# Fourteen transposes of the attention result moved from TensorE to DMA, in an attention and token-mixing kernel on one core

## The chip, the cores and the metric

The kernel runs on one core of a Trainium2 chip. The metric is the time of one execution on the device in microseconds (us), lower is better. Time before: a median of 142.5 us over three runs (142.19 to 142.66).

The engines are TensorE (PE in the profile; its weight loads are shown apart as PEld), VectorE (DVE), ScalarE (ACT), GpSimd (POOL) and SyncE (SP). In this kernel PE does all matrix work, ACT and DVE share what reads PE's results out of PSUM, POOL only issues loads once its constants are built, and SP only issues transfers: a few loads at the start, and all stores. A transfer is issued by an engine's queue in the order of the program and lands some microseconds later.

## The reference

Eight batches, eight heads, 576 tokens, 64 numbers per head. First an attention over a window of 128 tokens, with a bias that falls with the distance; then, on its result `x` of 576 x 512 per batch, a token-mixing layer:

```python
scores = scale * np.matmul(q, k.transpose(0, 1, 3, 2))
mask = (rel >= 0) & (rel < window)                 # rel = query position - key position
scores = np.where(mask, scores + bias[None], -1000000000.0)
attn = np.exp(scores - np.max(scores, axis=-1, keepdims=True))
attn = attn / (np.sum(attn, axis=-1, keepdims=True) + 1e-09)
x = np.matmul(attn, v)                             # heads side by side: batch x 576 x 512
...
wq = x @ w_q                                       # 512 -> 64
wk = x @ w_k                                       # 512 -> 64
W_tok = scale * np.einsum('bsd,btd->bst', wq, wk)
mixed = np.einsum('bst,btd->bsd', W_tok, x)
out = np.maximum(mixed, 0.0) @ w_out               # 512 -> 512
```

Inputs and output are in float32. The kernel works in float16 between PSUM sums.

## The kernel before

**The stages.** Every piece of work is an operation with a short name, a batch and a part. "Part" is a block of 128 tokens (0 to 3; 4 is the tail of 64 tokens) or a group of keys.

For each batch:
- Lq, Lk, Lv load a block of 128 tokens of q, k or v, all heads, from POOL (lines 378 and 391), changing float32 to float16 on the way. Lt loads the 64-row tails of q and k of two batches at once, into the tile natt (line 385).
- TQ transposes a block of q and of k on PE (eight transposes into one PSUM bank); ETQ copies the result to SBUF, on ACT or DVE. TT and ETT do the same with the tails. For batch 0, TF, TJ, EF and EJ stand for them.
- QK multiplies q and k for one group of keys and half of the heads; EXP takes the exponential (ACT, line 591); MUL multiplies by the bias and mask (DVE, line 598). There are 64 of each.
- PV multiplies by v, with a column of ones that gives the sum of each row; RC takes the reciprocal of the sums and X scales by it, which writes the tile x (DVE, lines 652 and 638). Part 4 of two batches shares one tile.

For each group of two batches (0 and 1, 2 and 3, 4 and 5, 6 and 7; operations are named by the first batch):
- XT transposes two x tiles, 128 tokens by 512 each, on PE: eight transposes of 128 x 128 (line 669). EXT copies them into the tile xT (line 675), on ACT or DVE. There are two XT and two EXT for each batch, sixteen in all. XTT and EXTT do the tail.
- WQ, WK and WT multiply xT by the weights; EWQ, EWK and EWT copy the results. WQ and WK of a group need all xT tiles of both batches.
- G forms the 64 x 512 product of wk and x, which replaces the token by token matrix; EG copies it. MX multiplies by wq, RM applies the relu (RMT for the tail), OUT multiplies by w_out, EO copies to an output buffer (tile osb, 15 buffers in rotation), and DO stores it from SP (lines 875 and 878).

CW and CWQ change weights to float16. WM are matmuls on zeros at the start, for the clock.

**The order.** Nothing is left to a scheduler. The string ORDER (lines 48 to 129) lists every operation with the engine that does it and its PSUM bank; each engine executes its own operations in that order, and waits for what an operation depends on. GT entries mark a place after which SP holds the next store back until a given QK is done. The numbers given to `add` (`want` and the engine costs) describe an operation for whoever makes the order; they are not read when the kernel is built.

**What surrounds XT.** X of an even and an odd block come first, then XT, EXT, and WK and WQ behind. An x tile has four buffers by batch (`NX`), so batch 4 overwrites the buffers of batch 0; `add_pv` therefore makes X wait for the XT of four batches before, and `add_xt` makes EXT wait for the WQ and WK of the batch whose xT buffer it overwrites. PE is in order, so an XT that waits for its X holds up whatever follows it on PE.

**Queues.** Both DMA queues use eight semaphores in rotation: each load of POOL, and each transfer of SP, waits for the landing of the one eight before it in the same queue.

Of the kernel before, what the change touches and what calls it, by code (L numbers as in the profile page):

```python
# [45 lines left out]
WARM = (13, 2, 5, 7, 5, 10, 2, 4, 4, 2, 1, 1, 2, 3, 4, 5, 1, 1, 2, 10, 1, 2, 2)  # L46

ORDER = """
warm:D LF0.0.1.1:A LF0.1.0.0:S iota:G WM.0:P01 ident:G wmc:D LF0.0.0.1:S LF0.0.1.0:A ones:D
mask:G LF0.0.0.0:S LF0.1.0.1:S Lq0.2:G bias:A Lk0.1:G zeros:D TF0.1.0:P00 Lt0:G WM.1:P10  # L50
TF0.0.1:P01 EF0.1.0:A biasl:D TF0.0.0:P10 TF0.1.1:P00 WM.2:P20 Lk0.3:G EF0.0.0:A QK0.0.0:P1
EF0.1.1:D Lq0.3:G WM.3:P20 EF0.0.1:D EXP0.0.0:A idh:D Lk0.2:G QK0.0.1:P0 TJ0.2.0:P20 EXP0.0.1:A
TJ0.1.1:P21 EJ0.2.0:D Lk1.3:G WM.4:P30 EJ0.1.1:D MUL0.0.0:D QK0.1.1:P0 Lq1.3:G QK0.1.0:P1
EXP0.1.1:A WM.5:P30 Lq1.2:G EXP0.1.0:A MUL0.1.1:D TT0:P00 Lk1.2:G WM.6:P30 ETT0:D ETT1:A
TJ0.3.1:P01 Lk1.1:G MUL0.1.0:D WM.7:P30 EJ0.3.1:A MUL0.0.1:D TJ0.3.0:P00 Lq1.1:G WM.8:P30
EJ0.3.0:A TJ0.2.1:P01 Lk1.0:G QK0.3.0:P1 EJ0.2.1:D WM.9:P30 EXP0.3.0:A QK0.2.1:P0 Lq1.0:G
WM.10:P30 QK0.3.1:P2 WM.11:P30 EXP0.2.1:A TQ1.3:P10 Lk2.3:G WM.12:P11 ETQ1.3:D EXP0.3.1:A
QK0.2.0:P3 WM.13:P11 Lv0.0:G MUL0.2.1:D TQ1.2:P00 EXP0.2.0:A Lv0.1:G QK1.3.0:P1 ETQ1.2:D
WM.14:P20 EXP1.3.0:A MUL0.3.1:D Lv0.2:G QK1.2.0:P0 TQ1.1:P30 MUL0.2.0:D EXP1.2.0:A Lk2.2:G
QK1.2.1:P1 ETQ1.1:D WM.15:P20 EXP1.2.1:A Lv0.3:G MUL1.2.0:D QK1.1.1:P0 TQ1.0:P30 MUL1.3.0:D  # L60
EXP1.1.1:A Lq2.2:G QK1.1.0:P1 ETQ1.0:D WM.16:P31 QK1.3.1:P2 EXP1.1.0:A WM.17:P31 Lq2.3:G
MUL0.3.0:D PV0.0:P0 QK1.0.0:P3 MUL1.1.1:D EXP1.3.1:A Lv1.0:G MUL1.2.1:D QK1.0.1:P1 EXP1.0.0:A
Lv1.1:G MUL1.1.0:D PV0.1:P2 RC0.0:D EXP1.0.1:A Lv1.2:G X0.0:D PV0.2:P3 RC0.1:D Lk2.0:G X0.1:D
PV0.3:P0 WM.18:P11 RC0.2:D X0.2:D Lv1.3:G TQ2.2:P10 XT0.0:P11 MUL1.3.1:D ETQ2.2:A Lq2.0:G
TQ2.3:P20 MUL1.0.1:D WM.19:P21 ETQ2.3:A Lq2.1:G MUL1.0.0:D RC0.3:D EXT0.0:A PV1.1:P3 X0.3:D
Lk2.1:G QK2.2.0:P2 pads:D PV1.2:P0 RC1.1:D Lv0.4:G EXP2.2.0:A X1.1:D XT0.1:P10 Lv1.4:G wz:D
RC1.2:D QK2.2.1:P3 Lw:S EXT0.1:A X1.2:D PV1.0:P2 Lk3.1:G WM.20:P11 Lwo.2:S RC1.0:D PV1.3:P0
EXP2.2.1:A X1.0:D Lwo.0:S Lq3.1:G WM.21:P11 Lwo.1:S RC1.3:D XT1.0:P10 Lwo.3:S X1.3:D Lt1:G
TQ2.0:P11 EXT1.0:A XT1.1:P00 ETQ2.0:D WM.22:P20 TQ2.1:P01 EXT1.1:D Lq3.0:G PV0.4:P1 ETQ2.1:D
PV1.4:P2 RC0.4:D Lk3.0:G X0.4:D QK2.1.1:P0 QK2.0.0:P3 EXP2.1.1:A Lk3.2:G RC1.4:D QK2.0.1:P1  # L70
X1.4:D Lq3.2:G CWQ:A MUL2.2.1:D QK2.1.0:P0 EXP2.0.0:A XTT0:P20 WK0:P21 Lq4.1:G EXTT0:D
MUL2.1.1:D EXP2.0.1:A Lk3.3:G WT0:P20 EWK0:D WQ0:P30 EWT0:A MUL2.0.0:D Lv2.1:G EXP2.1.0:A G0:P31
EWQ0:D CW.2:A CW.0:D TQ3.1:P10 EG0:A Lq3.3:G CW.1:A ETQ3.1:D MX0.0:P0 MX0.2:P2 RM1.0:A TT2:P11
RM0.2:D RM0.0:A MX0.3:P3 Lt2:G RM1.2:D RM1.3:A MX0.1:P0 ETT2:D RM0.3:A TQ3.0:P10 CW.3:D RM1.1:A
RM0.1:D QK2.3.1:P2 Lv2.0:G OUT1.1:P30 EXP2.3.1:A ETQ3.0:D Lv3.0:G TQ3.2:P31 EO1.1:A MUL2.3.1:D
QK3.0.1:P0 QK2.3.0:P2 Lv2.2:G ETQ3.2:D DO1.1:S EXP3.0.1:A OUT0.3:P10 ETT3:D Lq4.0:G MUL2.0.1:D
EXP2.3.0:A QK3.0.0:P3 QK3.1.1:P0 MUL2.1.0:D Lk4.0:G GT3.0:S OUT1.3:P11 EO0.3:A MUL2.3.0:D
EXP3.1.1:A Lv2.3:G TQ3.3:P20 MUL2.2.0:D OUT1.0:P21 EXP3.0.0:A ETQ3.3:D Lv3.1:G OUT0.1:P10
MUL3.0.1:D EO1.0:A MUL3.0.0:D EO1.3:A QK3.1.0:P0 QK3.3.0:P3 Lk4.1:G MUL3.1.1:D EXP3.1.0:A
QK3.3.1:P2 GT3.1:S GT3.3:S OUT0.2:P11 EO0.1:D Lv3.4:G EXP3.3.0:A MUL3.1.0:D PV2.1:P0 Lv3.2:G  # L80
OUT1.2:P10 EXP3.3.1:A RC2.1:D MUL3.3.0:D Lv3.3:G PV2.2:P3 X2.1:D EO1.2:A QK3.2.1:P2 EO0.2:A
Lv2.4:G RC2.2:D PV2.0:P0 DO1.2:S X2.2:D EXP3.2.1:A OUT0.0:P10 DO0.3:S Lk4.2:G RC2.0:D X2.0:D
TT4:P11 EO0.0:A Lk4.3:G MUL3.3.1:D MX0.4:P3 QK3.2.0:P2 ETT5:A RMT0:D PV3.1:P0 Lq4.3:G GT3.2:S
EXP3.2.0:A XT2.0:P10 MUL3.2.1:D PV2.3:P3 Lq4.2:G RC3.1:D EXT2.0:A MUL3.2.0:D TQ4.0:P20
OUT1.4:P21 RC2.3:D Lq5.3:G X3.1:D ETT4:A ETQ4.0:A X2.3:D PV3.0:P1 TQ4.1:P00 RC3.0:D PV3.2:P3
EO1.4:A X3.0:D Lq5.1:G ETQ4.1:A XT2.1:P01 RC3.2:D X3.2:D XT3.0:P10 Lq5.2:G PV3.3:P2 EXT2.1:A
EXT3.0:D PV3.4:P3 Lq5.0:G RC3.3:D QK4.0.0:P1 X3.3:D PV2.4:P0 Lk5.1:G EXP4.0.0:A GT4.0:S DO1.0:S
RC3.4:D XT3.1:P20 DO1.3:S RC2.4:D Lk5.2:G X2.4:D TQ4.3:P21 EXT3.1:A QK4.0.1:P1 X3.4:D Lk5.3:G
TQ4.2:P00 EXP4.0.1:A WK2:P01 ETQ4.2:D Lk5.0:G ETQ4.3:A XTT2:P20 QK4.1.1:P1 Lk6.3:G EXTT2:D
WQ2:P30 EXP4.1.1:A EWK2:D Lv4.1:G MUL4.0.0:D WT2:P31 EWQ2:D QK4.2.1:P2 EWT2:A QK4.1.0:P0  # L90
EXP4.2.1:A MUL4.1.1:D G2:P10 Lv4.2:G GT4.1:S MUL4.0.1:D EXP4.1.0:A Lk6.2:G QK4.2.0:P3 EG2:D
TQ5.1:P11 EXP4.2.0:A GT4.2:S DO1.4:S Lv4.0:G MX2.0:P0 ETQ5.1:D MX2.2:P2 DO0.1:S RM2.0:A MX2.1:P3
RM3.2:D Lk6.0:G RM3.0:A TQ5.2:P10 RM2.2:D TQ5.3:P11 RM2.1:A Lv4.3:G MUL4.1.0:D RM3.1:A MX2.3:P0
QK4.3.1:P2 RM3.3:A Lq6.0:G ETQ5.3:D TQ5.0:P30 EXP4.3.1:A OUT3.0:P31 ETQ5.2:D Lv5.2:G MUL4.2.0:D
RM2.3:A QK5.3.0:P1 QK5.2.0:P2 ETQ5.0:D EXP5.3.0:A GT5.3:S OUT2.3:P00 GT5.2:S EO3.0:D Lk6.1:G
EXP5.2.0:A OUT3.1:P01 MUL4.3.1:D DO3.0:S MUL4.2.1:D Lv5.1:G EO2.3:A QK5.0.1:P1 QK4.3.0:P3
MUL5.3.0:D EXP5.0.1:A QK5.0.0:P2 Lv4.4:G GT4.3:S OUT2.0:P00 EO3.1:D GT5.0:S EXP4.3.0:A
MUL5.0.1:D Lq6.2:G PV4.2:P1 OUT3.3:P01 EXP5.0.0:A RC4.2:D Lq6.1:G X4.2:D PV4.0:P3 EO2.0:A
MUL4.3.0:D QK5.1.0:P1 QK5.1.1:P2 EO3.3:A RC4.0:D GT5.1:S OUT2.1:P00 Lv5.0:G X4.0:D EXP5.1.1:A
DO3.3:S MUL5.2.0:D TQ6.0:P01 Lq6.3:G EXP5.1.0:A MUL5.1.1:D PV4.1:P3 OUT2.2:P20 Lv5.3:G RC4.1:D  # L100
ETQ6.0:A X4.1:D PV4.3:P1 Lv5.4:G MUL5.1.0:D EO2.2:A QK5.2.1:P3 RC4.3:D Lq7.1:G QK5.3.1:P2
EXP5.2.1:A X4.3:D OUT3.2:P01 MUL5.0.0:D Lk7.0:G EXP5.3.1:A PV4.4:P1 MUL5.2.1:D TQ6.2:P30 Lk7.1:G
RC4.4:D EO3.2:A MUL5.3.1:D XT4.1:P31 ETQ6.2:A PV5.2:P2 X4.4:D Lq7.0:G TQ6.1:P01 EO2.1:A EXT4.1:D
Lt3:G MX2.4:P1 XT4.0:P30 RMT2:A DO2.1:S RC5.2:D TQ6.3:P00 X5.2:D DO2.2:S ETQ6.1:A PV5.1:P1
DO3.2:S ETQ6.3:D DO2.0:S PV5.0:P2 EXT4.0:A Lv6.1:G OUT3.4:P31 RC5.1:D RC5.0:D X5.1:D Lk7.2:G
X5.0:D QK6.0.1:P0 EO3.4:A PV5.3:P1 EXP6.0.1:A Lq7.2:G XT5.0:P20 RC5.3:D X5.3:D PV5.4:P3 EXT5.0:A
Lv6.0:G QK6.1.1:P0 RC5.4:D QK6.2.0:P1 X5.4:D EXP6.1.1:A XT5.1:P21 Lq7.3:G TQ7.1:P20 EXT5.1:D
EXP6.2.0:A Lk7.3:G QK6.2.1:P3 QK6.0.0:P0 MUL6.0.1:D WK4:P21 GT6.0:S EXP6.0.0:A ETQ7.1:D Lv6.3:G
XTT4:P10 MUL6.2.0:D TQ7.0:P11 EXP6.2.1:A QK6.1.0:P0 ETQ7.0:D WQ4:P20 EWK4:A GT6.1:S EXTT4:D
EXP6.1.0:A MUL6.1.1:D WT4:P21 Lv6.2:G MUL6.2.1:D EWQ4:A QK7.0.1:P3 TT6:P10 MUL6.1.0:D EWT4:A  # L110
Lv7.1:G QK7.0.0:P0 EXP7.0.1:A G4:P11 MUL6.0.0:D GT7.0:S DO3.4:S Lv7.0:G ETT6:D EXP7.0.0:A
DO3.1:S QK6.3.1:P2 DO0.2:S EG4:D Lv7.4:G TQ7.2:P30 GT6.2:S EXP6.3.1:A DO0.0:S ETT7:D Lv7.2:G
MX4.2:P0 ETQ7.2:D MX4.3:P1 RM4.2:A MX4.0:P2 RM4.3:D Lv7.3:G RM5.3:A PV6.1:P3 RM5.0:D RM4.0:A
MX4.1:P1 RM5.2:A MUL7.0.0:D Lv6.4:G TQ7.3:P20 RM4.1:A RC6.1:D QK6.3.0:P0 ETQ7.3:D RM5.1:A
OUT4.1:P21 EXP6.3.0:A X6.1:D QK7.2.1:P1 EO4.1:D QK7.3.1:P3 EXP7.2.1:A QK7.2.0:P0 MUL6.3.1:D
OUT5.0:P20 DO4.1:S GT7.2:S GT6.3:S DO2.3:S MUL6.3.0:D EXP7.2.0:A PV6.2:P1 MUL7.0.1:D OUT4.0:P21
EXP7.3.1:A RC6.2:D X6.2:D QK7.1.1:P0 EO5.0:A QK7.3.0:P3 MUL7.3.1:D QK7.1.0:P1 EXP7.1.1:A
OUT5.1:P20 MUL7.2.0:D EXP7.1.0:A MUL7.2.1:D OUT4.2:P00 MUL7.1.1:D EXP7.3.0:A PV6.3:P1 MUL7.1.0:D
OUT4.3:P01 RC6.3:D EO4.0:A X6.3:D EO5.1:A PV7.1:P3 DO4.0:S MUL7.3.0:D EO4.2:A DO5.0:S PV6.0:P1
PV7.2:P2 GT7.1:S EO4.3:A RC6.0:D DO4.2:S RC7.1:D X6.0:D XT6.1:P00 DO5.1:S OUT5.3:P01 DO4.3:S  # L120
RC7.2:D EXT6.1:A X7.1:D GT7.3:S X7.2:D PV7.0:P1 EO5.3:A PV7.3:P3 RC7.0:D XT6.0:P00 X7.0:D
DO5.3:S PV6.4:P2 EXT6.0:A RC7.3:D X7.3:D XT7.0:P01 PV7.4:P1 RC6.4:D EXT7.0:A X6.4:D XT7.1:P30
# [48 lines left out]
def kernel(  # L171
# [111 lines left out]
    def pe(cols, tail=0.0):  # L283
        return {"PE": (cols, cols + 0.17 + tail)}
# [668 lines left out]
```

## Time and profile before

| | |
|---|---|
| median of the runs | 142.5 us (142.19 to 142.66, three runs) |
| the profiled execution, its own time | 142.51 us |
| its span in the profile | 140.4 us |
| busy: PE, DVE, ACT, POOL | 131.1, 117.0, 117.8, 95.6 us |
| last load issued, last landed | 107.0 us, 116.2 us |
| granted TensorE clock | 0.994 |

The page of the profile cuts the span into 40 slices and gives the busy share of each in tenths:

```profile
PE   6999998999898999999999999999899999999970
...
DVE  5866399998998999998899999989979999759330
ACT  4868899697599999998899999999989997748340
POOL 7999999999939998999969688996297000000000
PEclk9999999999999999999999999999999999999997
DMA  4999999999999999999999999999999979205593
```

The slices are 3.5 us each. POOL's row ends at slice 31, with the last load. DMA's row falls soon after. The four rows of the engines are all high from slice 12 on; the last five slices are the output matmuls of the last group, with little for DVE and ACT.

The profiled execution is 142.51 us by the device, and 140.4 us from its first to its last instruction in the profile; the times of the prediction's steps are on the profile's axis, from the span's start.

### The profile page before, as it was taken

What the parts mean: (1) busy time and instruction counts of PE and PEld (TensorE: products, weight loads), DVE (VectorE), ACT (ScalarE), POOL (GpSimd) and SP (SyncE); (2) the same over time, 40 slices, a digit from 0 to 9 for tenths busy, and PEclk for the clock granted to TensorE, in tenths of its full rate; (3) what the DMA queues carried; (4) which work ended last, traced back from release to release, by engine and by line L of the source; (5) the groups of instructions that cost most, each with busy time, mean ns of one, the idle gap of its engine ahead of it and who ended that gap; (6) DMA issues with size and microseconds to landing.
All of it is one profiled execution on the core that took longest, in us unless ns stands there. A gap on an engine that the chain in (4) does not pass through costs nothing.

```text
span 140.4 us, 4614 instructions
## 1 busy us (share of the span) xinstructions
PE 131.1 (93%) x1909; PEld 87.7 (62%) x1909; DVE 117.0 (83%) x270; ACT 117.8 (84%) x168; POOL 95.6 (68%) x118
## 2 busy tenths in 40 slices
PE   6999998999898999999999999999899999999970
PEld 5867655868664556788646566978446568753430
DVE  5866399998998999998899999989979999759330
ACT  4868899697599999998899999999989997748340
POOL 7999999999939998999969688996297000000000
PEclk9999999999999999999999999999999999999997
DMA  4999999999999999999999999999999979205593
GB/s 101 199 151 155 150 151 155 150 152 165 258 225 158 159 195 155 185 212 157 237 161 183 212 197 191 161 216 259 163 170 247 211 169 374 79 0 149 161 389 130
DMA packets 119477, 25.60 MB, mean 182 GB/s; under 512 B 114208, under 2 KB 114464, under 8 KB 119456
## 3 DMA queue, kind: packets, MB, share of 16 engines
q0 software_dynamic: 109264, 13.77, 154.7%
q1 hardware_dynamic: 9136, 11.28, 24.2%
q10 hardware_dynamic: 1056, 0.26, 0.8%
q8 instruction: 15, 0.25, 0.6%
q14 instruction: 6, 0.05, 0.1%
HBM read 29.62 MB, written 9.44 MB: 278 GB/s over the span
## 4 chain that ended last, share of the span: by engine, by line
PE 60%; ACT 15%; DMA 7%; DVE 6%; issue 5%; POOL 3%; ACTq 0%
PE pair L248 49%; PE pair L251 11%; ACT pt L591 10%; DMA natt<-in_k_dram 7%; POOL nat L378 2%; ACT rm L785 2%; DVE qkT L257 2%; DVE pt L598 1%; DVE x L638 1%; DVE osb L257 1%; ACT wout_sb L255 1%; ACT xT L255 1%; DVE inv L652 1%; POOL natt L385 1%; ACT wkt L255 0%
## 5 line engine op out<-in xcount | busy, mean ns | idle before, releaser
L591 ACT ACTIVATE pt<-pair 128x1024 f16<-128x1024 f32 x64 | 62.4, 1045 | 5.1 <-PE pair L248 5.0
L391 POOL DMA_DIRECT2D vt<-in_v_dram x40 | 34.7, 896 | 7.9 <-DMA natt<-in_q_dram 4.5
L598 DVE TENSOR_TENSOR pt<-pt,bias 128x1024 f16<-128x1024 f16 x48 | 31.6, 685 | 1.1 <-ACT pt L591 0.9
L248 PE MATMUL pair<-wout_sb,rm 128*128 128x512 f16 (+1 forms) x132 | 31.4, 373 | 0.0
L378 POOL DMA_DIRECT2D nat<-in_k_dram x31 | 28.8, 945 | 1.5 <-issue 0.5
L378 POOL DMA_DIRECT2D nat<-in_q_dram x30 | 28.1, 968 | 1.7 <-DMA vt<-in_v_dram 0.9
L248 PEld LDWEIGHTS <-pt 128*128 128x128 f16 x576 | 20.8, 97 | 5.8 <-issue 2.5
L248 PE MATMUL pair<-vt,pt 128*128 128x65 f16 x576 | 23.1, 193 | 0.9 <-ACT pt L591 0.8
L248 PE MATMUL pair<-qkT 64*128 64x256 f16 (+2 forms) x320 | 22.4, 250 | 0.8 <-ACT pt L591 0.3
L638 DVE TENSOR_TENSOR x<-pair,inv 128x512 f16<-128x512 f32 x32 | 21.7, 686 | 0.8
L257 DVE COPY qkT<-pair 128x1024 f16<-128x1024 f16 (+1 forms) x28 | 16.8, 611 | 5.3 <-PE pair L251 3.2
L255 ACT COPY osb<-pair 128x512 f32<-128x512 f32 (+1 forms) x28 | 15.9, 609 | 3.8 <-PE pair L248 3.8
L251 PE MATMUL pair<-identh,nat 128*128 128x128 f16 x244 | 18.8, 219 | 0.2
L248 PEld LDWEIGHTS <-rm 128*128 128x128 f16 x132 | 11.4, 97 | 12.0 <-issue 1.3
L251 PEld LDWEIGHTS <-nat 128*128 128x128 f16 x244 | 14.7, 98 | 3.8 <-issue 2.3
L248 PEld LDWEIGHTS <-qkT 64*128 64x128 f16 x320 | 10.9, 94 | 9.2 <-issue 4.0
L248 PE MATMUL pair<-warm 128*128 128x256 f16 x89 | 15.2, 299 | 1.1 <-DVE warm L298 1.1
L255 ACT COPY xT<-pair 128x1024 f16<-128x1024 f16 x12 | 12.1, 1023 | 1.7 <-PE pair L251 1.7
L255 ACT COPY qkT<-pair 128x1024 f16<-128x1024 f16 (+1 forms) x13 | 10.9, 866 | 1.7 <-PE pair L251 1.2
L785 ACT ACTIVATE rm<-pair 128x512 f16<-128x512 f32 x21 | 10.9, 623 | 0.0
L598 DVE TENSOR_TENSOR pt<-pt,biasl 128x1024 f16<-128x1024 f16 x16 | 10.8, 679 | 0.1
L248 PEld LDWEIGHTS <-warm 128*128 128x128 f16 x89 | 8.4, 106 | 4.0 <-issue 1.3
(69 smaller groups left out, 136.9 us busy)
## 6 DMA issues: line engine op xcount, KB each, us to landing
out_dram<-osb SPq DMA_DIRECT2D x31, 256.0 KB, 5.3
vt<-in_v_dram POOLq DMA_DIRECT2D x32, 128.0 KB, 6.9
nat<-in_k_dram POOLq DMA_DIRECT2D x31, 128.0 KB, 6.9
nat<-in_q_dram POOLq DMA_DIRECT2D x30, 128.0 KB, 6.9
out_dram<-osb SPq DMA_DIRECT2D x10, 128.0 KB, 2.5
osb<-in_moe_w_out_dram SPq DMA_DIRECT2D x4, 256.0 KB, 6.5
osb<-in_q_dram SPq DMA_DIRECT2D x4, 128.0 KB, 3.3
natt<-in_q_dram POOLq DMA_DIRECT2D x4, 128.0 KB, 8.1
```

Source lines behind the costliest of these rows:

```text
L248: hold(nc.tensor.matmul(*a, **k))
L251: hold(nc.tensor.transpose(*a))
L255: hold(nc.scalar.copy(out_ap, in_ap))
L257: hold(nc.vector.tensor_copy(out=out_ap, in_=in_ap))
L378: return lambda: nc.gpsimd.dma_start(out=natv(b, j, n), in_=(q, k)[j][b, :, P * n:P * n + P, :].transpose([1, 0, 2]))
L385: nc.gpsimd.dma_start(out=natt_s[pr % 2][:, j].rearrange("p e h d -> p (e h) d"), in_=(q, k)[j][2 * pr:2 * pr + 2, :, 512:576, :].rearrang ...
L391: return lambda: nc.gpsimd.dma_start(out=vtv(b, t)[:n, :, 0:D], in_=v[b, :, P * t:P * t + n, :].transpose([1, 0, 2]))
L591: nc.scalar.activation(out=pt[:, 0:1024], in_=two(s.bank).rearrange("p e c -> p (e c)"), func=AF.Exp, scale=SCALE)
L598: ENG2[o.eng].tensor_tensor(out=pt[:, 0:1024], in0=pt[:, 0:1024], in1=bt, op=ALU.mult)
L638: nc.vector.tensor_tensor(out=x[r].rearrange("p (g h d) -> p g h d", g=2, h=4), in0=sums(p)[r, :, :, 0:64], in1=box["inv"][r].unsqueeze(3) ...
L652: nc.vector.reciprocal(out=box["inv"][r], in_=sums(p)[r, :, :, 64])
L785: hold(nc.scalar.activation(out=out_ap, in_=in_ap, func=AF.Relu, scale=WSCALE))
```

## The change

For seven pairs of x tiles the XT on PE and the EXT on ACT or DVE are replaced by two DMA transposes each, DX, issued by SP: both pairs of batches 4, 5 and 6, and the first pair of batch 7. A DX reads one x tile (128 tokens by 512, float16, 128 KB) from SBUF and writes its four 128 x 128 blocks, transposed, straight into the xT tile in SBUF, without PSUM. It waits for the X of its tile alone. WQ and WK now wait for both DX of a pair in place of one EXT. Nine of sixteen XT and EXT stay as they were. The diff without most of the order:

```diff
-WARM = (13, 2, 5, 7, 5, 10, 2, 4, 4, 2, 1, 1, 2, 3, 4, 5, 1, 1, 2, 10, 1, 2, 2)
+DT = ((4, 0), (4, 1), (5, 0), (5, 1), (6, 0), (6, 1), (7, 0))
+
+WARM = (15, 8, 5, 8, 5, 2, 15, 1, 10, 7, 1, 3, 4, 4, 1, 1)
...
-        old = [gdn.get(GROUP.get(b - NX)), xtd.get((b - NX, qt // 2))]
+        old = [gdn.get(GROUP.get(b - NX)), xtd.get((b - NX, qt // 2)), xtd.get((b - NX, qt // 2, 0))]
...
     def add_xt(b, i, want):
+        if (b, i) in DT:
+            for n in range(2):
+                t = 2 * i + n
+
+                def dx(o, t=t):
+                    nc.sync.dma_start(out=xT_s[b % NX][:, :, P * t:P * t + P], in_=x_s[b % NX][t],
+                                      transpose=True)
+
+                old = [f(gi) for gi in (GROUP.get(b - NX),)
+                       for f in (lambda z: wqd.get((z, 0)), wkd.get)]
+                d = add("DX", b, t, want, {"SP": (0.6, 2.5)}, [xop[b, t], *old], dx)
+                xtd[b, i, n] = d
+            xtd[b, i] = d
+            ext[b, i] = [xtd[b, i, 0], d]
+            return
+
...
-        ext[b, i] = add("EXT", b, i, want + 0.6, EV(1.02, 0.69), [t, *old], ev, frees=[t])
+        ext[b, i] = [add("EXT", b, i, want + 0.6, EV(1.02, 0.69), [t, *old], ev, frees=[t])]
...
-        t = add("WQ", bs[0], "", want, pe(0.5 * nb), [wts, *(ext[b, i] for b in bs for i in range(2))],
+        t = add("WQ", bs[0], "", want, pe(0.5 * nb), [wts, *(e for b in bs for i in range(2) for e in ext[b, i])],
...
-                [wts, *(ext[b, i] for b in bs for i in range(2))], emk, banks=1)
+                [wts, *(e for b in bs for i in range(2) for e in ext[b, i])], emk, banks=1)
```

The whole of ORDER is new, from the first operation on: which engine does which copy, the sequence on every engine, the loads' sequence on POOL and the stores' place on SP. Its two places around the new transposes, DX4.1 to DX5.3 and DX6.1 to DX7.0, with what stands between the last of them and WK6:

```text
PV4.2:P1 RC4.1:D EO2.2:A X4.1:D QK5.0.1:P0 Lv5.3:G EO3.2:A MUL5.2.0:D QK4.3.0:P3 DX4.1:S
EXP5.0.1:A OUT2.1:P20 RC4.2:D Lq7.1:G X4.2:D EXP4.3.0:A PV4.0:P0 MUL5.0.1:D Lk7.0:G DX4.2:S
...
X5.0:D PV5.3:P0 Lq7.2:G ETQ6.3:A TQ7.1:P30 RC5.3:D DX5.0:S X5.3:D QK6.0.0:P2 QK6.2.0:P1
EXP6.0.0:A ETQ7.1:D TQ7.0:P31 Lq7.3:G GT4.3:S DX5.3:S MX2.4:P0 ETQ7.0:D EXP6.2.0:A QK6.1.0:P2
MUL6.0.0:D QK6.1.1:P3 GT5.3:S DO0.0:S EXP6.1.1:A RMT2:D QK6.2.1:P1 MUL6.2.0:D TT6:P00 EXP6.2.1:A
Lv6.0:G PV5.4:P3 ETT7:D ETT6:D EXP6.1.0:A Lv6.2:G QK7.0.1:P1 RC5.4:D PV4.4:P0 X5.4:D EXP7.0.1:A
Lv7.3:G QK7.0.0:P2 RC4.4:D OUT3.4:P30 X4.4:D EXP7.0.0:A MUL6.1.1:D XTT4:P31 Lv7.1:G QK6.3.1:P1
EXTT4:D QK6.0.1:P0 EXP6.3.1:A QK6.3.0:P2 EO3.4:D Lv7.0:G WT4:P31 MUL7.0.0:D WK4:P30 DO3.4:S
...
DX6.3:S X6.0:D EO4.3:A QK7.3.0:P2 OUT5.1:P11 EXP7.3.0:A RC7.0:D MUL7.3.1:D DX6.0:S X7.0:D
PV7.2:P3 EO5.1:A OUT5.3:P10 MUL7.3.0:D DX7.0:S RC7.2:D PV7.3:P0 X7.2:D EO5.3:A PV7.4:P2 RC7.3:D
DO2.0:S X7.3:D PV6.4:P3 DO4.0:S RC7.4:D MX4.4:P1 DO5.1:S X7.4:D XT7.1:P00 RMT4:A GT6.0:S GT6.3:S
GT6.1:S GT5.1:S GT6.2:S DO4.3:S OUT5.2:P01 EXT7.1:A RC6.4:D X6.4:D OUT5.4:P10 XTT6:P00 EO5.4:D
WK6:P11 EXTT6:A WT6:P00 EWK6:A WQ6:P20 EWT6:D EO5.2:D G6:P21 EWQ6:D DO5.2:S DO5.4:S OUT4.2:P30
```

SP issues its transfers in this order: in front of DX4.1 stand all stores of batch 1 and two of batch 0; behind DX5.3 come the eleven remaining stores of batches 0, 2 and 3, of which DO2.0 is the last and stands behind DX7.0. Before the change, SP issued its stores between 47 and 137 us, and nothing else after 35 us. The tail load of batches 6 and 7, Lt3, is the 92nd and 93rd transfer of POOL (94th and 95th before).

## The prediction

> **What bounds the kernel now.** I read the busy time by stretch first, then the chain of waits, then the load queue, then the groups that the change touches. Busy time of each engine in ten-microsecond stretches (stretch, length, then PE, weight loads, DVE, ACT, POOL, each with its instructions; granted clock, DMA share, GB/s):
>
> ```profile
> 80.00:90.00 10.00, 9.97 (x163) 7.10 (x163) 9.64 (x20) 9.94 (x14) 8.57 (x10) 1.00 2.23 185
> 90.00:100.00 10.00, 10.00 (x193) 7.48 (x194) 9.01 (x19) 9.71 (x13) 7.02 (x9) 1.00 2.03 216
> 100.00:110.00 10.00, 9.22 (x130) 5.46 (x130) 8.97 (x18) 9.47 (x17) 6.52 (x8) 1.00 2.02 202
> 110.00:120.00 10.00, 10.00 (x181) 7.22 (x178) 9.79 (x23) 9.02 (x14) 0.00 (x0) 1.00 1.17 262
> ```
>
> Three engines are full at once, at full clock. From 40 to 120 us PE is busy 78.3 of 80, ACT 77.0, DVE 75.2. Relief of one is worth only what the next allows. The chain of waits (start, length, what):
>
> ```profile
> 90.17 0.81 POOL natt L385
> 90.98 10.46 DMA natt<-in_k_dram
> 101.44 0.05 issue
> 101.48 0.35 PE pair L251 x6
> ...
> 106.83 9.66 PE pair L248 x136
> 116.49 0.45 PE pair L251 x8
> 116.94 1.60 PE pair L248 x28
> 118.53 0.45 PE pair L251 x8
> ```
>
> It passes through a load (the 64-row tails of batches 6 and 7, tile natt, which TT6 transposes) and then runs on PE; "L251 x8" behind 116 us is one XT, 0.45 us. POOL, in order of time, shows why loads matter (start, length, what, idle before and what ended it):
>
> ```profile
> 90.98 0.84 POOL L385 DMA_DIRECT2D natt<-in_k_dram  x1
> ...
> 99.90 0.87 POOL L391 DMA_DIRECT2D vt<-in_v_dram  x1 [2.41 <-DMA natt<-in_q_dram]
> 102.04 5.74 POOL L391 DMA_DIRECT2D vt<-in_v_dram  x7 [1.26 <-DMA natt<-in_k_dram]
> ```
>
> A load is issued every 0.9 us and waits for the load eight before it. Its place in the queue, not the engine work, sets when it lands. The last is issued at 107 us.
>
> **The parts, costed.** The rows of what goes and of what stands near it:
>
> ```profile
> L251 PE MATMUL pair<-identh,x 128*128 128x128 f16 x128 | 9.6, 219 | 0.1
> L255 ACT COPY xT<-pair 128x1024 f16<-128x1024 f16 x12 | 12.1, 1023 | 1.7 <-PE pair L251 1.7
> L257 DVE COPY xT<-pair 128x1024 f16<-128x1024 f16 x4 | 2.7, 684 | 0.1
> L638 DVE TENSOR_TENSOR x<-pair,inv 128x512 f16<-128x512 f32 x32 | 21.7, 686 | 0.8
> ```
>
> Removed: 7 XT, 56 of 128 transposes, 7 x 0.45 = 3.2 us of PE; 7 EXT, five on ACT (5 x 1.02 = 5.1 us) and two on DVE (2 x 0.68 = 1.4 us). Added: 14 DMA transposes of 128 KB in SP's queue. The written order deals other copies anew, and what counts is the work ahead of X7.3, the last full tile, behind which the kernel drains. Counting the two orders up to X7.3:
> - PE: 6 XT fewer (2.7), one OUT fewer (0.86): 3.6 us less.
> - DVE: two EXT, two ETQ and one EG fewer (5 x 0.68), one ETT and one EXTT fewer (2 x 0.42); two RM, one EO (3 x 0.68) and one CW (0.42) more: 1.8 us less.
> - ACT: four EXT fewer (4.1), two EO, two RM and one CW fewer (5 x 0.61); two ETQ more (2.0), an EG, ETT and EXTT more (3 x 0.6): 3.3 us less.
>
> The smallest saving decides where all three are full: DVE's 1.8. The same count can be read on the old time axis: I look up when the old execution had done as much of an engine's work as stands ahead of an operation in the new order, and take the latest engine. X7.3 ended at 119.9; the new order gives PE 116.0, DVE 118.2, ACT 116.2, so 118.2. Then PE does XT7.1 (0.45), OUT5.2, OUT5.4 (0.86 each) and XTT6 (0.22), and WK6 starts at 120.6 instead of 122.2. Behind WK6 both orders leave 13 us of PE (OUT4.2 stands where OUT5.4 filled the wait for EG6). Gain 1.6 us.
>
> The front part is reordered too (batch 1's loads ahead of the last of batch 0, 90 warm-up matmuls for 89). G0 ended at 42.0 and comes out at 42.1, so nothing is taken for it; bounds 1 us either way.
>
> DMA transposes: the old trace has none. Two things are to be bounded, the time to landing and the spacing in which one follows another. Issues and landings, 84 to 104 us, then 112 to 124 us:
>
> ```profile
> out_dram<-osb SPq DMA_DIRECT2D x6, 256.0 KB, 6.6
> ...
> out_dram<-osb SPq DMA_DIRECT2D x2, 128.0 KB, 5.2
> natt<-in_q_dram POOLq DMA_DIRECT2D x1, 128.0 KB, 9.4
> natt<-in_k_dram POOLq DMA_DIRECT2D x1, 128.0 KB, 10.5
> ```
> ```profile
> out_dram<-osb SPq DMA_DIRECT2D x6, 256.0 KB, 2.3
> ```
>
> Landing: 5.2 us beside the loads (equal bytes, same queue), upper end 10.5; 2.3 us after them. The last transpose of batches 4 and 5 follows X5.3 (93.5 by the count), WK4 is due at 99.7: 6.2 us of cover, 1.0 to spare; at 10.5 it is 4.3 late. DX7.0 follows X7.0 (116.2), WK6 is due at 120.6: 4.4 us of cover for 2.3. The cover is PE work: OUT3.4 and eight QK there, PV7.3, PV7.4, PV6.4, XT7.1 and two OUT here. Spacing: SP's stores follow one another in 0.4 us, and landed 0.6 to 0.8 us apart after the loads, 1.1 us apart beside them; a transpose has half their bytes in smaller pieces. I take 1.1 us, nearest by queue and size; lower end 0.4, upper end 2.5 (the page's median landing of a 128 KB store, if none overlaps). At 1.1 us, 14 of them are hidden; SP does nothing else.
>
> The Trainium skill speaks against the change: the page "VectorE: DVE Perf Modes", section "The three transpose paths", gives a 128x128 transpose 390 ns on TensorE and 1309 ns by DMA, and advises TensorE where PSUM will do. The first figure isn't what this chain shows (0.45 us for eight, 56 ns each). By the second, as an estimate, a tile's four blocks in a row are 5.2 us; "Advanced Engine Details and Errata", section "X-Bar Transpose (TRN2)", sets them instead near the speed of plain copies, which would leave the sum as it is.
>
> SP's queue: eight transposes now stand ahead of eleven stores of batches 0, 2 and 3. In the old trace six of these, 256 KB each, left between 77.8 and 91.6 us; now they wait for X5.3, and leave beside the last loads of batch 7. So stores leave the loads alone earlier, eight transposes of 128 KB take their place, and the stores come back behind them: I count that as nothing, bounds 3.5 us either way (8 x 0.43, half the issue time of a load, which moves twice the bytes). There are 15 output buffers; the nearest reuse is EO4.2, which needs DO2.0, queued behind DX7.0: issued at 117, landed at 119.5, wanted near 123. If SP ran 3.5 us late, EO4.2 would wait, behind it on ACT RM6.2, and behind that the nine last OUT.
>
> Loads: the tail load stands two places earlier in POOL's queue, so 1.9 us earlier, but TT6 comes at 95.4 instead of 100.5. At the page's median landing for natt (8.0) it lands at 97.1; EXP6.2.1 and EXP6.1.0 carry ACT to 98.4, and QK7.0.1 is through by 98.3. I charge 0.3 us.
>
> Sum: 142.51 (the profiled execution, span 140.4, in line with the median 142.5) - 1.6 + 0.3 = **141.2 us**.
>
> **The rivals.**
> - Tail loads late (no change). Lt3 took 10.5 us in the old trace. Then it lands at 99.5, QK7.0.1 ends at 100.7, ACT stands 2.3 us from 98.4, less the 0.7 us that PE waited before: 141.2 - 0.3 + 1.6 = 142.5. For it: that very row. Against: four 256 KB stores were issued within a microsecond of it, which now wait.
> - Transposes too close to one another (slower). Eight from X4.1 (84.5) to WK4 (99.7) and six from X6.1 (109.1) to WK6 (120.6) allow 1.9 us each. Above that SP's stream sets the end. At 2.5 us they end at 104.5 and 124.1, 4.8 and 3.5 late: 141.2 + 8.3 = 149.5; at 2.2 us, 145.3. For it: nothing in the trace shows a transpose overlapping another. Against: all other transfers of this queue overlap.
> - Four blocks of 128x128 to a tile, one after another (much slower), each at the spacing of a store: 4 x 1.1 = 4.4 us a tile beside the loads, 4 x 0.7 = 2.8 after. Eight end 35.2 us after 84.5, 20.0 late; six end 16.8 us after 109.1, 5.3 late: 166.5. Against it: each transpose is one instruction with one semaphore. By the skill's 1309 ns ("VectorE: DVE Perf Modes", as above) this rival would give some 187 us.
> - PE alone sets the end: all 3.2 us come, 139.3. Against it DVE's 9.79 of 10 in 110 to 120 us.
> - The change not doing what it says: the new order names 14 transposes on SP and 9 XT on PE; nothing is left to doubt.
>
> **How the numbers follow.** Forecast 0.51, its own range 140.3 to 142.0; tail loads 0.19; spacing 0.19; blocks in series 0.03; PE alone 0.08. A measurement here tells 0.3% (0.43 us) from no change, so faster is under 142.07, slower over 142.93. Faster: 0.48 of the forecast, 0.08, and 0.04 of the tail loads, 0.60. Same: 0.03 and 0.09, 0.12. Slower: 0.06, 0.19 and 0.03, 0.28. The range runs from 139.3 (PE alone) to 146.0 (2.2 us of spacing and some more); left out are about half of the spacing case, the blocks in series, and little below.
>
> **What would show it.** Right: DX landings under 6 us beside the loads and near 2.3 after, X7.3 ended near 118, PE without a gap at WK4 and WK6, DVE fuller than before from 100 to 118 us. Wrong: PE idle at WK4 or WK6, ended by a DMA into xT; DX landings spaced over 1.9 us; PE waiting several us for natt at TT6, or ACT idle behind it; EO4.2 waiting for a store.

## The result, and the profile after

The changed kernel takes 148.13 us (median of four runs, 146.91 to 149.17) against 142.52 us: it is 5.6 us slower. Two executions lasted 147 us at a granted clock of 0.994 to 1.0 and two 149 us at 0.985 to 0.987; the slowest is the profiled one (149.17 us, span 147.4), so a microsecond or two of its trace are not part of the comparison, and the ratio, 1.037 with a 95% interval of 1.027 to 1.047, leaves it out (the median of the other three is 147.23 us).

The 40 slices of the page of the changed kernel, 3.7 us each, in tenths:

```profile
PE   7899999867998999999999999989679989999990
...
PEclk9999999999999999999999999999977999999998
DMA  4999999999999999999999999999999999766994
```

Counted from 0, PE has a hole in two places: early, in slices 8 and 9 (29 to 37 us), and in slices 28 and 29 (103 to 110 us). The granted clock falls to 0.7 in slices 29 and 30. DMA stays full to slice 33, 125 us; before it fell behind 119 us. The stretches of ten microseconds show the second hole in numbers (columns as in the prediction):

```profile
90.00:100.00 10.00, 9.31 (x178) 7.19 (x176) 9.72 (x20) 8.82 (x12) 8.16 (x11) 1.00 2.25 129
100.00:110.00 10.00, 7.57 (x130) 4.91 (x128) 7.36 (x16) 7.65 (x12) 5.01 (x6) 0.94 1.81 158
110.00:120.00 10.00, 9.00 (x106) 4.79 (x104) 7.08 (x14) 6.89 (x11) 0.68 (x1) 0.89 1.80 246
```

From 100 to 110 us all three engines idle for more than two microseconds each, so none of them is the bound there. The chain of waits says what is (start, length, what):

```profile
91.99 0.70 POOL nat L379
92.69 10.59 DMA vt<-in_v_dram
103.56 15.55 DMA vt<-in_v_dram
119.16 8.35 PE pair L249 x156
```

Before, this part of the chain passed through one load and came back to PE at 101 us. Now it stays in two loads, one after another, until 119. A load of v that is issued at 103.56 lands 15.6 us later. The transfers issued from 84 to 112 us (KB each, median time to landing), and the first of these lines in the kernel before:

```profile
vt<-in_v_dram POOLq DMA_DIRECT2D x9, 128.0 KB, 13.4
nat<-in_q_dram POOLq DMA_DIRECT2D x5, 128.0 KB, 5.7
...
xT<-x SPq DMA_TRANSPOSE x8, 8.3
```
```profile
vt<-in_v_dram POOLq DMA_DIRECT2D x9, 128.0 KB, 8.4
```

And the packets that the two queues moved from 90 to 110 us, before the change and after it (q0 carries the loads, q1 SP's transfers; packets, MB, share of the engines):

```profile
q0 software_dynamic: 17267, 2.18, 171.8%
q1 hardware_dynamic: 1087, 1.96, 29.4%
```
```profile
q0 software_dynamic: 12507, 1.58, 147.5%
q1 hardware_dynamic: 4272, 1.26, 54.9%
```

In the same 20 us 4760 fewer load packets went through, 4.6 loads at 1024 packets each, although SP moved fewer bytes than before (1.26 MB for 1.96). It moved them in four times as many packets: a transposed tile counts 512 packets of 256 B and 32 of 4 B. The last load landed at 121.5 us; before it was 116.2.

PE's own longest wait for a transfer is for a transpose, and the load of the chain shows with a shorter one (PE's timeline: start, length, idle before in brackets):

```profile
104.50 1.01 PE L249 MATMUL pair<-wqk_sb,xT 128*128 128x64 f16 x28
107.93 0.29 PE L249 MATMUL pair<-wqk_sb,xT 128*128 128x64 f16 x4 [2.42 <-DMA xT<-x]
...
119.16 0.66 PE L249 MATMUL pair<-vt,pt 128*128 128x65 f16 x16 [0.72 <-DMA vt<-in_v_dram]
```

The 28 matmuls of WK4 run, and the last four wait for DX5.3. X5.3 was done at 96.9, but DX5.0 held SP for 3.1 us; DX5.3 was issued at 99.5 and landed at 107.9. The two waits stand for the same time in part. Where the loads are fewer (below), PE comes to the matmul of the last line at 114.5; here it came at 118.4, because of DX5.3 and the clock behind it, and stood 0.7 us more. The load, issued at 103.56 before either wait, would have held it until 119.2 without them.

Ahead of the transposes the kernel is late too: the matmuls of G0 ended at 44.3 us (41.7 before), X3.3 at 66.8 (64.5). X7.3 ended at 127.3 (119.9 before, 118.2 forecast).

### The profile page after: what moved, and what is told of

The parts are those of the page before. It is cut to its first block, busy times and chain, and to the rows that moved or that the text cites. A ratio compares the mean times of both kernels' runs of the same rounds, so it can differ in the third digit from the quotient of the medians.

```text
span 147.4 us, 4515 instructions
## 1 busy us (share of the span) xinstructions
PE 133.3 (90%) x1854; PEld 86.8 (59%) x1854; DVE 116.6 (79%) x268; ACT 115.4 (78%) x163; POOL 95.6 (65%) x118
## 4 chain that ended last, share of the span: by engine, by line
POOL 29%; PE 25%; DMA 24%; DVE 8%; ACT 8%; issue 4%; POOLq 0%; ACTq 0%; DVEq 0%
PE pair L249 22%; POOL nat L379 18%; DMA vt<-in_v_dram 18%; POOL vt L392 8%; DMA nat<-in_q_dram 6%; ACT pt L592 3%; PE pair L252 3%; POOL natt L386 2%; DVE pt L599 2%; ACT xT L256 2%; DVE x L639 2%; ACT osb L256 1%; DVE rm L804 1%; ACT qkT L256 1%; DVE wout_sb L258 1%
## 5 line engine op out<-in xcount | busy, mean ns | idle before, releaser
L258 DVE COPY qkT<-pair 128x1024 f16<-128x1024 f16 (+1 forms) x25 | 15.0, 612 | 9.2 <-PE pair L252 8.9
L252 PE MATMUL pair<-identh,nat 128*128 128x128 f16 x244 | 19.3, 222 | 0.4 <-DMA nat<-in_q_dram 0.2
L256 ACT COPY osb<-pair 128x512 f32<-128x512 f32 (+1 forms) x26 | 14.5, 593 | 5.6 <-PE pair L249 4.0
L256 ACT COPY qkT<-pair 128x1024 f16<-128x1024 f16 (+1 forms) x16 | 13.6, 863 | 3.0 <-PE pair L252 3.0
L249 PE MATMUL pair<-warm 128*128 128x256 f16 x90 | 14.1, 298 | 1.4 <-DVE warm L299 1.1
L249 PEld LDWEIGHTS <-warm 128*128 128x128 f16 x90 | 8.9, 106 | 3.9 <-issue 1.3
L258 DVE COPY osb<-pair 128x512 f32<-128x512 f32 (+1 forms) x11 | 7.3, 663 | 3.8 <-PE pair L249 3.6
L802 ACT ACTIVATE rm<-pair 128x512 f16<-128x512 f32 x18 | 9.3, 622 | 0.6 <-PE pair L249 0.6
```

The lines of the kernel that those rows point to most:

```text
L249: hold(nc.tensor.matmul(*a, **k))
L252: hold(nc.tensor.transpose(*a))
L256: hold(nc.scalar.copy(out_ap, in_ap))
L258: hold(nc.vector.tensor_copy(out=out_ap, in_=in_ap))
L802: hold(nc.scalar.activation(out=out_ap, in_=in_ap, func=AF.Relu, scale=WSCALE))
```

## The experiments

Theory A: a DMA transpose costs no engine time but takes the place of about one load in flight; the loads of batches 6 and 7 come late, and the engines wait for them. Theory B: the new order, above all its front, costs the time, whatever does the transposes. In the diffs the first file is the kernel before unless another is named.

**The new order without DMA transposes.** All seven pairs go back to XT and EXT, in the changed kernel's order.

```diff
-DT = ((4, 0), (4, 1), (5, 0), (5, 1), (6, 0), (6, 1), (7, 0))
+DT = ()
```

> The new order with all 14 transposes taken back to PE: 7 XT and 7 EXT (five on ACT, two on DVE) stand where the second transpose of each pair stood. Theory A (the DMA transposes delay the loads beside them, whose landings grew from 5 to 16 us): with no transposes in flight the loads land as before, G4 ends near 106 instead of 112.1 us, and the time falls to 142.5 to 143.5. Theory B (the new order itself loses, since G0 ended 2.6 us and G2 4.2 us late before the first transpose was issued at 87.3 us): the time stays at 146 or more, and with the 3.2 us of PE back rather above 147. If both share the loss, 144 to 145.5.

Measured: 154.55 us (152.50 to 156.47). The loads issued from 84 us on landed in 4.5 to 6 us, the last at 108.8, yet PE waited for copies by ACT and DVE, with X5.3 at 100.3. Where the seven XT and EXT were put is my choice, and it broke the fit of the order; nobody's number was met. What follows is only that this order relies on having no XT there.

**The old order with all 14 transposes**, each right behind its X.

```diff
-RC4.1:D ETQ6.0:A X4.1:D PV4.3:P1 Lv5.4:G
+RC4.1:D ETQ6.0:A X4.1:D DX4.1:S PV4.3:P1 Lv5.4:G
```

> The order of before, with the same 14 DMA transposes, each put on SP right behind the X of its tile, and the 7 XT and 7 EXT taken out; nothing else moves. Theory A: the loads issued from 85 us on land late as in the changed kernel, 12 us and more, and the time is 145 to 147. Theory B: the transposes are hidden, PE, ACT and DVE have less to do, and the time is 141 to 142. Theory C (the last transposes come too late for WK4 and WK6, whatever the loads do): PE waits 2 us and more at WK4 or WK6 for xT, loads land in under 10.5 us.

Measured: 156.52 us (155.12 to 158.02), ratio 1.094 (1.086 to 1.103). Loads issued from 85 to 95 us took 11 to 17 us to land. The waits (us in total, times, longest):

```profile
PEld L251 <- DMA nat<-in_k_dram: 5.6, 1, 5.6
PE pair L251 <- DMA nat<-in_k_dram: 5.4, 1, 5.4
...
PEld L248 <- DMA xT<-x: 3.3, 1, 3.3
```

The larger wait is for a load of k, Lk7.1: it landed in time for TQ7.1, which began at 95.6 us before, and at 105.9 us here. The wait for a transpose, at WK6, is the smaller one. That speaks for A, and against B: the order is the old one.

**The two groups apart**, in the old order: the eight transposes of batches 4 and 5, and the six of batch 6 and 7.0.

```diff
+DT = ((4, 0), (4, 1), (5, 0), (5, 1))
```

> The order of before with 8 DMA transposes alone, those of batches 4 and 5, beside the loads of batches 6 and 7. Theory A: all of the loss of the variant with 14 is here, 144.5 to 147, with the loads issued from 85 to 100 us landing after 10 us and more. Theory B: 141 to 142.5. Theory C: PE waits for xT at WK4 while the loads land as before.

```diff
+DT = ((6, 0), (6, 1), (7, 0))
```

> The order of before with 6 DMA transposes alone, those of batch 6 and of the first pair of batch 7 (X6.1 is at 108 us, the last load is issued at 107). Theory A: hardly a load is left to delay, so the saving of 3 XT (1.4 us of PE) and 3 EXT (3.1 us of ACT) shows: 141 to 142. Theory C: WK6 waits for DX7.0, 143 to 144. Theory B says nothing against it: 141 to 142.

Measured: the eight 151.65 us (ratio 1.065, 1.058 to 1.072), the six 148.49 us (1.040, 1.033 to 1.047). The waits of the run with eight, then of that with six:

```profile
PEld L251 <- DMA nat<-in_k_dram: 6.7, 1, 6.7
```
```profile
PEld L248 <- DMA xT<-x: 3.8, 1, 3.8
```

The eight run beside loads, and Lk7.1 takes 16.8 us instead of 6.5. The six hardly touch the loads; there it is SP's queue. X7.0 was done at 120.0 us, but DX7.0 was issued only at 124.8, because DX6.0, two stores and DX7.1 stood ahead of it from 119.5 on, and DX7.1 alone held SP for 2.8 us; WK6, which began at 123, waited. The changed kernel's order avoids that: its WK6 waited for nothing.

All three runs in the old order cost more than Theory A or any other expectation said. One difference of the orders may explain part of it, and no run tests it alone: the changed kernel issues Lk7.1 at 76.7 us, ahead of the transposes, and the old order at 88 to 89 us, among them.

**Four transposes of batch 6 alone, stores behind them**, as a try at a faster version: DO4.0, DO5.0 and DO4.2 are put behind DX6.0.

```diff
+DT = ((6, 0), (6, 1))
...
-PV7.1:P3 DO4.0:S MUL7.3.0:D EO4.2:A DO5.0:S PV6.0:P1
+PV7.1:P3 MUL7.3.0:D EO4.2:A PV6.0:P1
...
+X6.0:D DX6.0:S DO4.0:S DO5.0:S DO4.2:S DO5.1:S
```

> The old order with only the four transposes of batch 6 on SP (X6.1 at 108 us, X6.0 at 117) and the stores DO4.0, DO5.0 and DO4.2 put behind the last of them; 2 XT (0.9 us of PE) and 2 EXT (2.0 us of ACT) are gone. With six transposes WK6 waited 3.7 us for the last, whose landing was held up on SP behind stores and other transposes. Theory A and C: here the last one lands at 120, ahead of WK6 at 122, and the time is 141.5 to 142.5, a chance to beat both kernels. If PE's own pace does not change because DVE sets the end there: 142.3 as before. If transposes lose even here: 144 and more.

Measured: 143.63 us (142.20 to 144.20, ten runs), ratio 1.007 (1.003 to 1.011). No wait was left at WK6, and yet nothing was gained: the two EXT that go were ACT's, and X7.3, a step of DVE, came at 120.5 us where it had come at 119.9. Where the small loss comes from is not shown.

**The old front with the new back**: the old order up to ETQ4.3, the changed kernel's from there.

> The old order up to ETQ4.3 (66 us, between the loads of batch 4 and WK2), the new order with its 14 transposes from there on; only five operations are out of the new order's sequence at the seam. The changed kernel ended G2 at 75.9 us, the one before at 71.7. Theory B (the new front of the order loses 4 us and the transposes then lose little more): about 143, that is 147.2 of the changed kernel's undisturbed runs less 4. Theory A (the transposes beside the loads lose it all, and the front's delay is only slack): 147 as the changed kernel.

Measured: 146.99 us (146.84 to 147.87), ratio 1.030 (1.024 to 1.036). G0 is back at 41.7 us, and little is won. The hole and the fallen clock stay (PE and PEclk in 40 slices of 3.6 us, then two of PE's waits):

```profile
PE   7999997999899999998969999985999979999990
...
PEclk9999999999999999999999999998699999999999
```
```profile
99.37 0.40 PE L251 MATMUL pair<-identh,natt 64*128 64x64 f16 x8 [1.04 <-DMA natt<-in_k_dram]
...
117.02 0.66 PE L248 MATMUL pair<-vt,pt 128*128 128x65 f16 x16 [1.00 <-DMA vt<-in_v_dram]
```

PE waits for no transpose in this run, neither at WK4 nor at WK6; its waits for transfers are all for loads, 2.5 us together from 98 us on (and 1.4 us at 74, ahead of the transposes). So the front is at most a small part of the 5.6 us while the loads are late.

**Eight transposes added that nobody reads**, to the kernel before, issued from 34 us on, and **eight plain copies** in their place, in 512 pieces of 256 B each.

```diff
+    for i in range(8):
+        def dd(o, i=i):
+            nc.sync.dma_start(out=xT_s[2 + i // 4][:, :, P * (i % 4):P * (i % 4) + P], in_=x_s[i // 4][i % 4], transpose=True)
```

> The kernel before, with eight added DMA transposes of 128 KB on SP right behind the weights' loads (issued from 35 us on), from x tiles of batches 0 and 1 into xT tiles of batches 2 and 3 that are written again later; nothing reads them. They only take queue and DMA time. Theory A: each displaces about one load (in the changed kernel 236 packets of transposes a us stood for 499 fewer load packets a us, 1075 load packets for a transpose of 512, a load has 1024): the loads behind them land 7 to 8 us later and the time is 147 to 150. If a transpose costs only its packets in the load's currency (half a load): 3 to 4 us later, 145 to 146.5. Theory B: no change, 142.5.

```diff
+            nc.sync.dma_start(out=xT_s[2 + i // 4][:, :, P * (i % 4):P * (i % 4) + P], in_=x_s[i // 4][i % 4].rearrange("p (c t) -> p c t", c=4))
```

> The same as the variant with eight added transposes, at the same place and with the same sources, bytes and number of 256-byte pieces, but as plain copies within SBUF, without transposing. If it is the number of pieces and bytes that displaces loads, the time and the landings are those of the eight transposes. If it is the transposing, the copies cost 2 us or less: 142.5 to 144.5.

Later the same copies in 128 pieces of 1 KB:

```diff
+            nc.sync.dma_start(out=xT_s[2 + i // 4][:, i % 4, :], in_=x_s[i // 4][i % 4])
```

> The kernel before with eight added copies of 128 KB at the same place as the eight dummy transposes, but in 128 pieces of 1 KB each rather than 512 of 256 B; nothing reads them. If the number of pieces is what displaces the loads (Theory A in its sharper form): a quarter of the pieces, so +1.6 to +2.5 us in place of +6.5 us. If the bytes moved decide: +6.5 us again.

Measured, each with its ratio to the kernel before, and the load Lk3.3, which all eight transfers overtake:

| added | time | more | ratio (interval) | Lk3.3 landed |
|---|---|---|---|---|
| nothing | 142.3 us | | | 47.6 us |
| 8 transposes | 150.65 | 8.3 us, 1.04 each | 1.053 (1.045 to 1.061) | 57.3 |
| 8 copies, 256 B | 148.80 | 6.5 us, 0.81 each | 1.044 (1.037 to 1.051) | 54.5 |
| 8 copies, 1 KB | 146.99 | 4.6 us, 0.57 each | 1.033 (1.026 to 1.040) | 51.4 |

No engine does any more work in these kernels, and nothing waits for the added transfers. The packets from 40 to 48 us, in the kernel before and in those with transposes, with 256 B and with 1 KB copies:

```profile
q0 software_dynamic: 9461, 1.19, 235.1%
q1 hardware_dynamic: 37, 0.06, 2.3%
```
```profile
q0 software_dynamic: 3717, 0.47, 106.5%
q1 hardware_dynamic: 1984, 0.51, 74.8%
```
```profile
q0 software_dynamic: 4162, 0.53, 101.0%
q1 hardware_dynamic: 2624, 0.81, 67.4%
```
```profile
q0 software_dynamic: 4565, 0.58, 112.0%
q1 hardware_dynamic: 1276, 1.26, 57.6%
```

In the first block the loads have the DMA engines to themselves. With transposes in flight 5744 load packets are missing for 1984 packets of SP's: one displaces 2.9. Lk3.3 slips by 9.7 us, and the kernel ends 8.3 us later. Theory A's price of a full load for a transpose is met. (PE waits for the late loads, and from 45 to 55 us its granted clock is 0.5 to 0.63; how much of the 8.3 us that makes is not separated. Lk3.3 was issued at 39.5 us, ahead of it.) The rival that bytes alone count falls, as fewer pieces of the same bytes cost less; but a quarter of the pieces costs 0.57 us and not a quarter, so the piece count is not all of it either, and the 1 KB run came out above the 1.6 to 2.5 us expected of it. The transposing itself is the smallest part, 0.2 us, and no more than a hint: the intervals of transposes and 256 B copies overlap.

**Six transposes that nobody reads, after the last load.**

```diff
-DO5.3:S PV6.4:P2 EXT6.0:A
+DO5.3:S DD.0:S DD.1:S DD.2:S DD.3:S DD.4:S DD.5:S PV6.4:P2 EXT6.0:A
```

> The kernel before with six added transposes of 128 KB behind the store DO5.3 (about 118.8 us), after the last load has landed (116.2 us); nothing reads them. Theory A (a transpose costs what it takes away from the loads in flight): no load is in flight, so no more than 0.5 us is lost, though SP is held for six times 1.2 us. Rival (a transpose costs about 1 us wherever it stands, by SP, by the memory's ports or by the clock): 6 x 1.04 = 6.2 us more.

Measured: 142.80 us (142.05 to 143.87, ten runs) against 142.39, ratio 1.004 (1.001 to 1.008). The issue timeline of SP and the page's line of landings:

```profile
118.43 8.82 SPq L932 DMA_TRANSPOSE xT<-x  x6
```
```profile
xT<-x SPq DMA_TRANSPOSE x6, 2.4
```

They hold SP for 8.8 us, 1.5 each, and cost 0.4 us together, not 6.2. So the price is not the transpose's own: it is what is in flight beside it, or waits for it.

**Fewer loads.** Batch 7's loads of q, k and v are cut from 128 partitions to 16, in the changed kernel, in the kernel before, and in the kernel with the old front and the new back; the rest of each tile keeps what an earlier batch left there, so batch 7's output is not the reference's.

```diff
+R = (128,) * 7 + (16,)
...
-            out=natv(b, j, n), in_=(q, k)[j][b, :, P * n:P * n + P, :].transpose([1, 0, 2]))
+            out=natv(b, j, n)[0:R[b]], in_=(q, k)[j][b, :, P * n:P * n + R[b], :].transpose([1, 0, 2]))
...
-        n = P if t < 4 else 64
+        n = min(R[b], P if t < 4 else 64)
```

> The changed kernel with batch 7's loads of q, k and v cut from 128 partitions to 16 (the rest of each tile keeps what an earlier batch left there, so batch 7's output differs): some 11 loads' worth of packets leave the stretch in which the transposes run. Theory A (the loads come late because the transposes' packets displace theirs): the loss of 5.6 us against before goes, 140.5 to 142.5 us. Rival (SP's held-up transposes, their own landing of 6 to 8 us and the clock make the loss): 145 us or more.

> The kernel before with the same cut of batch 7's loads, as the base for the run above. Both theories: before the change the loads are ahead of their use by a few us, so this gains little, 141 to 142.5 us.

> The order of the kernel before up to ETQ4.3, the changed kernel's order with its 14 transposes behind it, and batch 7's loads cut to 16 partitions as in the two runs with fewer loads. With the new front and the same cut the loss was 2.0 us. If that rest is the new front (G0 at 44.5 us in place of 42.0): at or below the kernel before with the same cut, 141.0 to 142.6 us, that is, the gain that was forecast or nothing. If the rest comes from the stretch with the transposes: 144 to 145 us again.

Measured, medians in us:

| | loads full | batch 7's loads cut |
|---|---|---|
| the kernel before | 142.5 | 142.45 (141.99 to 143.13) |
| the changed kernel | 148.13 (147.23 without the profiled run) | 144.47 (144.26 to 144.55) |
| old front, new back, 14 transposes | 146.99 | 142.75 (142.25 to 143.43) |

Before the change the cut is worth nothing: the loads were early enough. After it, it is worth 3.7 us (2.8 us from 147.23), and 4.2 us with the old front. These kernels run the same 14 transposes on the same queue. The 144.47 us lie between the two ranges that were expected, and the 142.75 us just above the lower one of theirs. The cut also lets the transposes land sooner (DX5.3 in 6.4 us and not 8.4), and the wait of WK4 for DX5.3 goes with it; so in the changed kernel the cut doesn't part late loads from late transposes. With the old front it does: PE waited for no transpose there even with the full loads, and with the cut the 2.5 us of waits for loads are gone, and so is the clock of 0.66 behind them. The 4.2 us go with those two; how much each makes is not parted. The second row against the third gives the front, 1.7 us with the cut. What is left, 142.75 against 142.45, is no gain and hardly a loss. The three steps, 0.3, 1.7 and 3.7 us, are differences along one row of medians, so that they add up to the whole proves nothing.

**The new front alone**: the changed kernel's order up to EWK2, the old one behind it, no transposes.

> The changed kernel's order up to EWK2, then that of the kernel before, and no DMA transposes at all. If the new front costs time by itself once nothing later hides it: 144 to 145.5 us (1.5 to 3 us more than before). If the front's 2.5 us at G0 are slack: 142 to 143 us.

Measured: 147.19 us (146.59 to 147.59), ratio 1.034 (1.029 to 1.039), above both expectations. X3.3 is 2.2 us late and G2 5.4 us; from G2 to the last copy it runs as fast as before (64.5 us for 65.1). The 3 us between X3.3 and G2 lie where I joined the two orders, so this run says that the front's delay is real (2.2 us at X3.3), but not that it is 4.9 us.

## Why the prediction was wrong

- **What bounds the kernel** (three engines full, the loads' place in the queue setting when they land): right, and the second half should have been given a price. That the loads had some room is shown by the cut, worth nothing before; that the room ends within 14 transposes by the cut afterwards.
- **The step that failed** is the one on SP's queue: "I count that as nothing, bounds 3.5 us either way (8 x 0.43, half the issue time of a load, which moves twice the bytes)". The price went by bytes. Measured in the run with eight added, a transpose beside loads costs 1.04 us, more than a whole load's issue time of 0.9 us and 2.4 times my bound. Eight of them came to 8.3 us where nothing was taken away for them. In the changed kernel six stores of 256 KB leave the same stretch, which I did not measure by itself; by the cut, 2.8 to 3.7 us of late loads and late transposes reach the end. That alone is about the bound. The rest of the way from 141.2 to 148.1 us are the front (1.7 us, taken as nothing) and the gain that did not come (1.5 us: 142.75 with old front and cut, for 141.2).
- **Landing and spacing.** Landing was taken as 5.2 us beside the loads, to 10.5; it was 8.3. DX5.3 landed 11.0 us after X5.3, 2.6 of them in SP's queue and 8.4 to landing, for 6.2 us of forecast cover; WK4 gave 8.6, and PE waited 2.4. After the loads 2.3 was forecast, and 2.4 is the median of the six late ones; the last six of the changed kernel itself, among stores, took 5.4 to 2.4. Spacing: 1.1 us was forecast. SP was held 1.2 to 1.5 us by most of them, but beside the loads the eight landed 2.1 us apart on average (93.4 to 107.9 us; 1.8 in the run with eight added). The Trainium skill's 1309 ns for a 128x128 block ("VectorE: DVE Perf Modes", "The three transpose paths") would be 5.2 us for a tile, as an estimate; a tile landed in 2.4 us on a free queue, so the blocks don't run one after another at that price. The Trainium skill's "Advanced Engine Details and Errata", section "X-Bar Transpose (TRN2)", sets a transpose near a plain copy; the runs come near that only for a copy in equally small pieces (1.04 against 0.81 us, and 0.57 us for pieces of 1 KB).
- **The front** was taken as nothing, bounds 1 us. It made G0 2.6 us late, and costs 1.7 us where the loads don't hide it (with the full loads 1.1 us between the medians, 0.2 us from 147.23). The changed kernel's chain has a load there (start, length, what):

```profile
29.87 8.93 DMA nat<-in_q_dram
38.85 0.64 PE pair L252 x8
```

  It is Lq2.0, for TQ2.0, issued at 29.9 and landed at 38.8 us; before, it was issued at 26.8 and landed at 32.1. PE stood only 0.1 us for it, though, and 2.2 us in five gaps for ACT and DVE between 29 and 37 us, so which of them makes the front late stays open. Counting work along the old time axis sees neither, as it counts no waits.
- **DVE's saving of 1.8 us** did not arrive. With the old front and the cut loads X7.3 came at 120.3 us, where 118.2 was forecast and 119.9 measured before. X5.3 came at 94.7 us, as before, for a forecast of 93.5, and the way from X5.3 to X7.3 took 25.6 us for one of 24.7. Engine counts give what an order could reach if it left no gaps; this one left some, and I did not isolate them. Behind X7.3 the step held: 16.6 us to the last copy for 16.5 before.
- **The rivals.** Tail loads late: Lt3 was not what decided. Transposes too close: its first half came. The landings of the eight were 2.1 us apart, over its limit of 1.9, and PE stood 2.4 us at WK4, as this rival has it at 2.2 us (84.5 + 8 x 2.2 = 102.1, for 99.7). Its second half did not: WK6 waited for nothing. That its 145.3 to 149.5 us hold the measured time is partly luck, as the late loads, the front and the missing gain are not in it. Blocks in series fall with the tile that landed in 2.4 us, and PE alone with the 142.75 us of the old front and fewer loads, where its 139.3 should have shown.

## What to carry to other kernels

Price a transfer by what it displaces on the queues beside it, in pieces as well as in bytes, and ask of every load behind it how many microseconds of room it has. Transposes given to DMA were nearly free where no load was in flight and nobody waited for them (0.4 us for six), and dear where loads were (8.3 us for eight) or where a reader waited for them behind the stores of the same queue (6.2 us for six in the old order). When all engines idle at once after a change that took work off them, read the landing times first.

## What was not expected of the hardware

- SP stays on a transpose for 1.2 us and more at issue, against 0.4 us for a store, so six in a row hold its queue for 8.8 us.
- A short idle of PE is followed by a lower granted clock: 0.66 from 100 to 105 us in the run with the old front, 0.7 in two slices of the profiled execution of the changed kernel. In the run with six transposes of batches 6 and 7 the last copy came 6.3 us late (142.8 for 136.5 us): 0.8 us ahead of WK6, 3.8 us of wait there, and the rest behind it, with the clock at 0.5 in one slice.
